# Reciprocals of the softmax sums: one transpose and copies by DMA in place of spread transposes and products

## The chip, the core and the metric

The kernel runs on one core of one Trainium2 chip. The core has five engines that run side by side, each in the order of its own instructions: TensorE (PE, with PEld for its weight loads), VectorE (DVE), ScalarE (ACT), GpSimd (POOL) and SyncE (SP, which here only issues DMA transfers). They wait for each other by semaphores. The metric is the device time of one execution in microseconds (us).

## What is computed

Attention with a position bias for 4 batches of 8 heads (576 tokens, 64 channels a head), then a first feed-forward layer with `g = h * cos(h)`, then a gated one with an RMS norm. The change lies in the attention:

```python
scores = scale * np.matmul(q, k.transpose(0, 1, 3, 2)) + bias
scores = scores - np.max(scores, axis=-1, keepdims=True)
attn = np.exp(scores)
attn = attn / (np.sum(attn, axis=-1, keepdims=True) + 1e-09)
return np.matmul(attn, v)
...
h = x @ w_in;  g = h * np.cos(h);  x = g @ w_out          # then RMS norm, SiLU gate, w_out
```

## The kernel before

**Units and steps.** The attention is cut into 16 units `u` (a pair of heads of one batch). A unit has five steps `p` = 0 to 4, and `step(u, p)` issues in this order: the score products of the step (`qk`, float32r, into the two PSUM tiles `psS`), then on VectorE `most` (adds the bias, takes the row's greatest value), then the transposes and copies of an earlier step, and on ScalarE `exps` (the exponential with the row sum). Steps 0 to 3 hold 128 query rows of each of the two heads, step 4 the last 64 rows of both heads together. That makes nine sums for a partition, `sum[:, 0:9]`.

**From scores to output.** `blocks` and `ninths` transpose the exponentials on TensorE into `pt` (three PSUM buffers), from where ScalarE and VectorE copy them to `eT`. `av(u, 0)` in step 3 multiplies them with `v` for the query rows of steps 0 and 1 ("half 0"), `av(w, 1)` in step 1 of the next unit (`w = u - 1`) those of steps 2 to 4 ("half 1"). The result `o` (one PSUM buffer) has channels on partitions and query rows along the free axis, 64 partitions for each head. So it can be divided by its sums only when 1/sum lies along the free axis too, the same in all 64 partitions of a head: this is the tile `rbc`. `norm_mul` multiplies `o` with `rbc` on VectorE: half 0 in `turn_end` (step 0 of the next unit), half 1 in step 2. `norm_split` then writes the two float32r parts `xh` (ScalarE) and `xl` (GpSimd).

**How rbc is made.** `recip(u, 0, 8)` in step 4 takes eight reciprocals on VectorE, and GpSimd widens each to 64 columns (`rw`, two copies). TensorE transposes `rw` in four pieces of 128x128 (L292), two in step 4 and two in the next step 0. `spread` copies each pair from PSUM to `rbc` on ScalarE (L308). The ninth reciprocal goes by `recip(u, 8, 9)` in `turn_end` and by two products with the identity (L319) ahead of `av(w, 1)`; `norm_tail` copies them (L342).

**What else stands near.** SP issues all loads in program order: `v` of the next unit (L361), weights `raw` for the later layers (L105, 512 KB, from unit 4), `rawk` and `rawq` of the next unit (`load`, L189), and in every fourth unit (3, 7, 11) nine bias loads (L215, L219). A DMA that waits for an engine holds all behind it on SP. The two layers that follow the attention (`run_item`) begin on TensorE at about 296 us.

Of the kernel before, what the change touches and what calls it, by code (L numbers as in the profile page):

```python
# [53 lines left out]
def attn_moe(tc, qd, kd, vd, smallp, lrow, ident_d, wf1, wf2, rmsg, out):  # L54
    nc = tc.nc
# [123 lines left out]

    raw_kq = {}  # L180

    def load(u):
        for k, src in enumerate((kd, qd)):
            if u == 0:
                t = rawp.tile([128, 512, 2], I32, tag="raw", name="first", bufs=NRAW)
                t = t.rearrange("p a b -> p (a b)")[:, 0:640].bitcast(F32)
            else:
                t = prep.tile([128, 640], F32, tag="raw" + "kq"[k], name="raw" + "kq"[k], bufs=1)
            nc.sync.dma_start(t, src[u % 4, u // 4])  # L189
            raw_kq[u, k] = t  # L190
        if u == 0:
            kq[0] = [raw_kq[0, 0], raw_kq[0, 1]]
# [70 lines left out]
    def exps(u, j):  # L263
        s_ = st[u]
        e2 = s_["e"][j // 2]
        e = e2[:, S * (j % 2):S * (j % 2) + S]
        nc.scalar.activation(e, e, AF.Exp, bias=s_["m"][:, j:j + 1], scale=-1.0, accum_out=s_["sum"][:, j:j + 1])  # L267
        if j == 8:
            nc.gpsimd.tensor_copy(e2[:, S:S + 64], e2[:, S - 64:S])
# [15 lines left out]
    def ninths(u, ps, half=None):  # L285
        s_ = st[u]
        pt = psA.tile([128, 512], F32, tag="tr", name="pt", bufs=3)
        for i, p in enumerate(ps):
            nc.tensor.transpose(pt[:, 128 * i:128 * i + 128], s_["e"].pop(p)[:, 512:640], ident)  # L289
        if half is not None:  # L290
            for i in range(0, 256, 128):
                nc.tensor.transpose(pt[:, 256 + i:384 + i], s_["rw"][:, 256 * half + i:256 * half + i + 128], ident)  # L292

        def out(copy):
            if ps[0] == 0:
                copy(s_["eT", 0][:, 8, 0:256], pt[:, 0:256])
            else:
                q0 = 128 * (ps[0] - 2)
                copy(s_["eT", 1][:, 8, q0:q0 + 128], pt[:, 0:128])

        def small(copy):
            for r0 in (0, 64):
                r = slice(r0, r0 + 64)
                copy(s_["eT", 1][r, 8, 256:320], pt[r, 128 + r0:192 + r0])

        def spread():
            rbc = ap.tile([128, 320], F32, tag="rbc", name="rbc", bufs=2)
            nc.scalar.copy(rbc[:, 0:256], pt[:, 256:512])  # L308
            s_["rbc", half] = rbc
        return out, small, spread  # L310

    def av(u, half):
        s_ = st[u]
        n = 256 if half == 0 else 320
        eT = s_["eT", half]
        o = s_["o"] = psA.tile([128, 512], F32, tag="o", name="o", bufs=1)
        if half == 1:
            for hh in range(2):
                nc.tensor.matmul(o[64 * hh:64 * hh + 64, 320:384], s_["r"][:, 8:9].to_broadcast([128, 64]),  # L319
                                 ident[:, 64 * hh:64 * hh + 64], start=True, stop=True, tile_position=(0, 64 * hh))  # L320
        vt = vts[u]
        for c in range(5):
            for hh in ((0, 1) if c % 2 else (1, 0)):
                nc.tensor.matmul(o[64 * hh:64 * hh + 64, 0:n], vt[:, c, 64 * hh:64 * hh + 64],  # L324
                                 eT[:, 2 * c + (hh if c < 4 else 0), :], start=(c == 0), stop=(c == 4),
                                 tile_position=(0, 64 * hh))

    def recip(u, a, z):  # L330
        s_ = st[u]
        nc.vector.tensor_scalar(s_["sum"][:, a:z], s_["sum"][:, a:z], 1e-9, None, op0=ALU.add)
        nc.vector.reciprocal(s_["r"][:, a:z], s_["sum"][:, a:z])
        if a == 0:
            rw = s_["rw"] = ap.tile([128, 512], F32, tag="rw", name="rw", bufs=1)
            for i in range(0, 8, 4):
                nc.gpsimd.tensor_copy(rw[:, 64 * i:64 * i + 256].rearrange("p (a b) -> p a b", b=64),
                                      s_["r"][:, i:i + 4].unsqueeze(2).to_broadcast([128, 4, 64]))

    def norm_tail(u):  # L340
        s_ = st[u]
        nc.scalar.copy(s_["rbc", 1][:, 256:320], s_["o"][:, 320:384])  # L342

    def norm_mul(u, half):
        s_ = st[u]
        n = 256 if half == 0 else 320
        xt = s_["xt"] = ap.tile([128, 320], F32, tag="xt", name="xt", bufs=1)
        nc.vector.tensor_tensor(xt[:, 0:n], s_["o"][:, 0:n], s_["rbc", half][:, 0:n], op=ALU.mult)

    def norm_split(u, half):  # L350
        hp, b = divmod(u, 4)
# [6 lines left out]
    def start_unit(u):  # L358
        hp, b = divmod(u, 4)
        vt = ap.tile([128, 5, 128], F32, tag="v", name="v", bufs=2)  # L360
        nc.sync.dma_start(vt, vd[b, hp])  # L361
        vts[u] = vt
        sm = ap.tile([128, 32], F32, tag="sm", name="sm", bufs=2)
        st[u] = {
            "m": sm[:, 0:9], "sum": sm[:, 10:19], "r": sm[:, 20:29], "e": {},
        }

    def turn_end(u, *now):
        a, b, c = blocks(u, 3, 0), blocks(u, 3, 1), blocks(u, 4, 0)
        out, small, spread = ninths(u, (3, 4), 1)  # L370
        recip(u, 8, 9)
        norm_mul(u, 0)
        a(nc.scalar.copy)
        if now:
            exps(now[0], 0)
        c(nc.scalar.copy)
        b(nc.vector.tensor_copy)
        out(nc.scalar.copy)
        small(nc.vector.tensor_copy)
        if now:  # L380
            exps(now[0], 1)
        spread()
        norm_split(u, 0)

    def convert(n):
# [4 lines left out]
    def step(u, p):  # L390
        hp, b = divmod(u, 4)
        w = u - 1
        if p == 0:
            start_unit(u)
        pss = qk(u, p)
        if p == 4:
            recip(u, 0, 8)
            if u >= 4:
                convert(1)
        for j, ps in enumerate(pss, 2 * p):  # L400
            most(u, j, ps)
            if b == 3:
                load_bias(hp + 1, j)
        if p == 0:
            if u >= 4:
                w_tick(lambda i: False)
            turn_end(w, u)
            if u > 1:
                split_q(u, 4)
            if u < 15:  # L410
                load(u + 1)
        elif p == 1:
            if w >= 0:
                av(w, 1)
            else:
                c0, c1 = blocks(u, 0, 0), blocks(u, 0, 1)
                c0(nc.vector.tensor_copy)
            exps(u, 2)
            exps(u, 3)
            if u == 0:  # L420
                c1(nc.scalar.copy)
            if u >= 4:
                convert(2)
            if w >= 0:
                norm_tail(w)
        elif p == 2:
            cs = [blocks(u, i, k) for i in range(1 if u == 0 else 0, 2) for k in range(2)]
            out, _, _ = ninths(u, (0, 1))
            if u >= 4:
                w_tick(lambda i: i < WA + WB, 1, False)  # L430
            cs.pop(0)(nc.scalar.copy)
            cs.pop(0)(nc.scalar.copy)
            exps(u, 4)
            if w >= 0:
                norm_mul(w, 1)
            for c in cs:
                c(nc.vector.tensor_copy)
            out(nc.scalar.copy)
            exps(u, 5)
            if 0 < u < 15:  # L440
                split_k(u + 1)
        elif p == 3:
            if 0 < u < 15:
                split_q(u + 1, 0)
            av(u, 0)
            if w >= 0:
                norm_split(w, 1)
            exps(u, 6)
            exps(u, 7)
            if u >= 4:  # L450
                convert(1)
        else:
            c0, c1 = blocks(u, 2, 0), blocks(u, 2, 1)
            out, _, spread = ninths(u, (2,), 0)
            if 0 < u < 15:
                split_q(u + 1, 1)
            c0(nc.scalar.copy)
            exps(u, 8)
            c1(nc.vector.tensor_copy)
            out(nc.scalar.copy)  # L460
            spread()
            if 0 < u < 15:
                split_q(u + 1, 2)
                split_q(u + 1, 3)
# [14 lines left out]
    nc.vector.memset(halfpi, float(math.pi / 2))  # L479
    nc.scalar.activation(cv[:, 0:1], halfpi, AF.Relu)  # L480
    nc.vector.memset(cv, 0.0)
    nc.vector.tensor_scalar(nbp, psi, b1s, -1.0, op0=ALU.mult, op1=ALU.mult)
    nc.gpsimd.tensor_scalar(w2s, w2s, 8.0, None, op0=ALU.mult)
    nc.scalar.activation(psb, psi, AF.Identity, scale=b1s)
# [347 lines left out]

    def rest():
        av(15, 1)
        norm_tail(15)

    turn_end(15)
    run_item(0, rest)
    def rest_out():
# [84 lines left out]
```

## Time and profile before

| what | value |
|---|---|
| median of 3 runs | 1150.82 us (1150.66 to 1151.09) |
| the profiled execution | 1150.9 us, its span in the trace 1149.1 us |
| mean granted TensorE clock | 0.999 of full speed |
| busy in the span | PE 1140.8, DVE 803.9, ACT 547.5, POOL 444.4 us |
| one unit in steady state | 15.5 us |

The span is what the trace covers; 1.8 us of the execution lie around it. A "busy" engine is one that has an instruction running; several TensorE instructions overlap in its pipeline, so what one costs is read from the start of it to the start of the next.

### The profile page before, as it was taken

To read this page: it belongs to the slowest core of one execution; us is meant where nothing else is said; L and a number is where in the kernel's file an instruction comes from. 1 tells how busy PE (TensorE), PEld (TensorE's weight loads), DVE (VectorE), ACT (ScalarE), POOL (GpSimd) and SP (SyncE) were. 2 spreads that over 40 slices of the span, in tenths; PEclk is the share of its full clock that TensorE was granted. 3 is DMA by queue.
4 is the path that set the end of the run, shared out by engine and by line. 5 is a ranking of instruction groups with operands and counts; after the bars stand their busy time and mean duration, and the time that the engine had idled before them with its cause. 6 is when DMAs were issued, how large, how long until landed. Compare 5 with 4: busy or idle time off the path is not lost.

```text
span 1149.1 us, 18558 instructions
## 1 busy us (share of the span) xinstructions
PE 1140.8 (99%) x6982; PEld 918.7 (80%) x6982; DVE 803.9 (70%) x1526; ACT 547.5 (48%) x1106; POOL 444.4 (39%) x555
## 2 busy tenths in 40 slices
PE   9999999999999999999999999999999999999998
PEld 4577777777788888888888887888888888888887
DVE  8867888888797798698778998685556355543232
ACT  8977788887653444354455555332322222122111
POOL 0245576665242352243244457553421241133111
PEclk9999999999999999999999999999999999999999
DMA  7925343442011011011101101011111011100111
GB/s 249 297 75 170 104 156 120 158 148 72 21 55 37 19 55 56 19 37 57 54 19 37 55 1 56 19 55 41 52 56 56 22 53 55 56 1 1 37 62 67
DMA packets 30682, 79.28 MB, mean 69 GB/s; under 512 B 3872, under 2 KB 4128, under 8 KB 30592
## 3 DMA queue, kind: packets, MB, share of 16 engines
q1 hardware_dynamic: 30400, 77.65, 21.4%
q8 instruction: 55, 0.90, 0.3%
q14 instruction: 35, 0.29, 0.1%
q10 hardware_dynamic: 144, 0.29, 0.1%
q0 software_dynamic: 48, 0.15, 0.1%
HBM read 62.47 MB, written 15.61 MB: 68 GB/s over the span
## 4 chain that ended last, share of the span: by engine, by line
PE 93%; ACT 2%; DVE 2%; POOL 1%; issue 1%; DVEq 0%; POOLq 0%; ACTq 0%
PE y L618 28%; PE h L618 17%; PE hv L618 12%; PE hg L618 12%; PE o L324 7%; PE psS L244 7%; PE pt L281 6%; PE psb L545 2%; ACT G L554 1%; PE pt L289 1%; PE pt L292 1%; DVE sq L734 0%; POOL wC L148 0%; PE o L319 0%; ACT ft L495 0%
## 5 line engine op out<-in xcount | busy, mean ns | idle before, releaser
L685 POOL TENSOR_TENSOR g<-t,g 128x512 fp32r<-128x512 f32 (+1 forms) x60 | 75.1, 1252 | 293.2 <-ACT g L684 293.2
L668 POOL TENSOR_TENSOR g<-t,g 128x512 fp32r<-128x512 f32 (+1 forms) x80 | 97.7, 1221 | 234.9 <-ACT g L667 234.9
L680 DVE TENSOR_TENSOR t<-t,hg 128x512 f32<-128x512 f32 (+1 forms) x60 | 38.0, 633 | 136.1 <-ACT t L679 136.1
L258 DVE CUSTOM_DVE_ANT_0 e<-psS,bias 128x576 f32<-128x576 f32 x144 | 103.9, 755 | 40.7 <-PE psS L244 35.0
L618 PE MATMUL y<-g,wB 128*128 128x512 f32 (+1 forms) x600 | 132.0, 369 | 0.0
L618 PEld LDWEIGHTS y<-g,wB 128*128 128x128 f32 x600 | 104.8, 189 | 19.1 <-POOL g L668 0.3
L267 ACT ACTIVATE e<-e,sm 128x576 f32<-128x576 f32 x144 | 112.0, 779 | 5.1 <-DVE sm L258 4.1
L679 ACT ACTIVATE t<-hg 128x512 f32<-128x512 f32 (+1 forms) x60 | 33.3, 554 | 169.2 <-PE hg L618 159.0
L684 ACT CAST g<-t 128x512 fp32r<-128x512 f32 (+1 forms) x60 | 34.7, 578 | 162.0 <-DVE t L683 162.0
L618 PE MATMUL h<-xh,wB 128*128 128x512 f32 (+1 forms) x360 | 109.1, 369 | 0.0
L618 PE MATMUL hv<-xh,wB 128*128 128x512 f32 (+1 forms) x320 | 97.2, 369 | 1.4 <-DVE t L666 1.4
L662 ACT ACTIVATE r<-r 128x512 f32<-128x512 f32 (+1 forms) x80 | 47.2, 589 | 105.7 <-DVE r L659 105.3
L618 PE MATMUL hg<-xh,wB 128*128 128x512 f32 (+1 forms) x320 | 96.8, 368 | 0.0
L618 PE MATMUL y<-wB,g 128*128 128x512 f32 x378 | 91.4, 389 | 0.0
L667 ACT CAST g<-t 128x512 fp32r<-128x512 f32 (+1 forms) x80 | 46.2, 578 | 94.6 <-DVE t L666 85.6
L324 PE MATMUL o<-eT,v 128*64 128x256 f32 (+1 forms) x640 | 83.9, 408 | 0.0
L618 PEld LDWEIGHTS y<-wB,g 128*128 128x128 f32 x378 | 70.5, 188 | 14.3
L244 PE MATMUL psS<-kt,qt 64*128 64x288 f32 (+1 forms) x810 | 79.7, 309 | 0.0
L618 PE MATMUL y<-g,wC 128*128 128x512 f32 (+1 forms) x360 | 79.7, 370 | 0.0
L244 PEld LDWEIGHTS psS<-kt,qt 64*128 64x128 f32 (+1 forms) x810 | 62.0, 185 | 20.7 <-issue 12.7
L683 DVE TENSOR_TENSOR t<-t,hv 128x512 f32<-128x512 f32 (+1 forms) x60 | 38.0, 633 | 57.6 <-PE hv L618 57.4
L666 DVE TENSOR_TENSOR t<-r,h 128x512 f32<-128x512 f32 (+1 forms) x80 | 50.3, 629 | 36.5 <-ACT r L663 36.1
(143 smaller groups left out, 2652.6 us busy)
## 6 DMA issues: line engine op xcount, KB each, us to landing
raw<-in_wf_dram SPq DMA_DIRECT2D x68, 512.0 KB, 3.6
bdram<-G SPq DMA_DIRECT2D x36, 295.5 KB, 4.6
bias<-bdram SPq DMA_DIRECT2D x32, 288.0 KB, 3.9
v<-in_vd_dram SPq DMA_DIRECT2D x16, 320.0 KB, 3.4
rawk<-in_kd_dram SPq DMA_DIRECT2D x15, 320.0 KB, 4.5
rawq<-in_qd_dram SPq DMA_DIRECT2D x15, 320.0 KB, 3.1
out_dram<-yacc SPq DMA_DIRECT2D x16, 256.0 KB, 2.1
bias<-bdram SPq DMA_DIRECT2D x4, 128.0 KB, 2.7
```

The costliest lines, as they stand in the source:

```text
L244: nc.tensor.matmul(ps[:, x, 0:288], qt[r, a, 128 * p:128 * p + 128], kt[r, b_, k0:k0 + 288], start=(n == 0), stop=(n == len(terms) - 1), t ...
L258: nc.vector.tensor_tensor_reduce(out=e.rearrange("p (a b) -> p a b", a=2), in0=ps[:, :, 0:288], in1=bias_t[j].rearrange("p (a b) -> p a b" ...
L267: nc.scalar.activation(e, e, AF.Exp, bias=s_["m"][:, j:j + 1], scale=-1.0, accum_out=s_["sum"][:, j:j + 1])
L281: nc.tensor.transpose(pt[:, 128 * i:128 * i + 128], e[:, k0:k0 + 128], ident)
L324: nc.tensor.matmul(o[64 * hh:64 * hh + 64, 0:n], vt[:, c, 64 * hh:64 * hh + 64], eT[:, 2 * c + (hh if c < 4 else 0), :], start=(c == 0), s ...
L618: nc.tensor.matmul(ps, a, b_, start=(first and k == 0), stop=(last and k == tot - 1))
L662: nc.scalar.activation(r, r, AF.Abs)
L666: nc.vector.tensor_tensor(t, r, ps, op=ALU.mult)
L667: nc.scalar.copy(g[:, 0, :tn], t)
L668: nc.gpsimd.tensor_tensor(g[:, 1, :tn], t, g[:, 0, :tn].bitcast(F32), op=ALU.subtract)
L680: nc.vector.tensor_tensor(t, t, pg, op=ALU.mult)
L685: nc.gpsimd.tensor_tensor(g[:, 1, :tn], t, g[:, 0, :tn].bitcast(F32), op=ALU.subtract)
```

## The change

Each half takes its reciprocals in one piece: `recip(u, 0)` (four sums, at the end of step 1) and `recip(u, 1)` (five sums, ahead of the next unit's step 0). They go into `rs[half]`, 16 or 20 columns with a reciprocal in every fourth. One transpose turns `rs[half]` to 16 or 20 rows of 128; it stands behind those of the exponentials in step 2 (half 0) and in the next step 0 (half 1). ScalarE copies these rows to `row`. SP then issues DMAs that read one row of `row` and write it to 64 partitions of `rbc[half]`: four for half 0, six for half 1. `load` is split, so that `rawk` is issued ahead of half 1's copies and `rawq` behind them. The widening on GpSimd, the four 128x128 transposes, the two products and their copies are gone.

```diff
-    def load(u):
-        for k, src in enumerate((kd, qd)):
+    def load(u, which=(0, 1)):
+        for k in which:
+            src = (kd, qd)[k]
...
         if half is not None:
-            for i in range(0, 256, 128):
-                nc.tensor.transpose(pt[:, 256 + i:384 + i], s_["rw"][:, 256 * half + i:256 * half + i + 128], ident)
+            n = 4 * (4 + half)
+            nc.tensor.transpose(pt[0:n, 256:384], rs[half], ident)
...
         def spread():
-            rbc = ap.tile([128, 320], F32, tag="rbc", name="rbc", bufs=2)
-            nc.scalar.copy(rbc[:, 0:256], pt[:, 256:512])
-            s_["rbc", half] = rbc
+            row = ap.tile([128, 128], F32, tag=f"row{half}", name="row", bufs=1)
+            nc.scalar.copy(row[0:n, :], pt[0:n, 256:384])
+            s_["row"] = row
...
-        if half == 1:
-            for hh in range(2):
-                nc.tensor.matmul(o[64 * hh:64 * hh + 64, 320:384], s_["r"][:, 8:9].to_broadcast([128, 64]),
-                                 ident[:, 64 * hh:64 * hh + 64], start=True, stop=True, tile_position=(0, 64 * hh))
...
+    rbc = [ap.tile([128, 256 + 64 * i], F32, name=f"rbc{i}") for i in range(2)]
+    rs = [ap.tile([128, 16 + 4 * i], F32, name=f"rs{i}") for i in range(2)]
...
+    def recip(u, half):
+        sums = s_["sum"][:, 4 * half:4 + 5 * half]
+        nc.vector.tensor_scalar(sums, sums, 1e-9, None, op0=ALU.add)
+        nc.vector.reciprocal(rs[half].rearrange("p (c z) -> p c z", z=4)[:, :, 0], sums)
...
+    def to_channels(u, half):
+        row = st[u]["row"]
+        for hh in range(2):
+            to = rbc[half][64 * hh:64 * hh + 64, :]
+            for p in range(2):
+                j = 4 * (2 * p + hh)
+                nc.sync.dma_start(to[:, 128 * p:128 * p + 128], row[j:j + 1, :].unsqueeze(1).to_broadcast([1, 64, 128]))
+            if half == 1:
+                nc.sync.dma_start(to[:, 256:320], row[16:17, 64 * hh:64 * hh + 64].unsqueeze(1).to_broadcast([1, 64, 64]))
...
     def turn_end(u, *now):
-        recip(u, 8, 9)
         norm_mul(u, 0)
...
         small(nc.vector.tensor_copy)
+        spread()
+        to_channels(u, 1)
         if now:
             exps(now[0], 1)
-        spread()
...
         if p == 0:
             start_unit(u)
+            if w >= 0:
+                recip(w, 1)
         pss = qk(u, p)
         if p == 4:
-            recip(u, 0, 8)
...
+            if u < 15:
+                load(u + 1, (0,))
             turn_end(w, u)
             if u > 1:
                 split_q(u, 4)
             if u < 15:
-                load(u + 1)
+                load(u + 1, (1,))
...
-            if w >= 0:
-                norm_tail(w)
+            recip(u, 0)
...
             out(nc.scalar.copy)
+            spread()
+            to_channels(u, 0)
             exps(u, 5)
...
+    for t in rs:
+        nc.vector.memset(t, 0.0)
```

On TensorE, from the last transpose of unit 1's step 4 to step 2 of unit 2, there stand before (`psS` scores, `pt` transposes, `o` the product with `v`):

```order
L289 MATMUL pt<-ident,e 128x128
L292 MATMUL pt<-ident,rw 128x128 x2
L244 MATMUL psS<-kt,qt 128x288 x12
L281 MATMUL pt<-ident,e 128x128 x12
L289 MATMUL pt<-ident,e 128x128 x2
L292 MATMUL pt<-ident,rw 128x128 x2
L244 MATMUL psS<-kt,qt 128x288 x12
L319 MATMUL o<-ident,sm 64x64 x2
L324 MATMUL o<-eT_1251,v 64x320 x10
L244 MATMUL psS<-kt,qt 128x288 x12
L281 MATMUL pt<-ident,e 128x128 x16
L289 MATMUL pt<-ident,e 128x128 x2
```

and at the same place after:

```order
L290 MATMUL pt<-ident,e 128x128
L245 MATMUL psS<-kt,qt 128x288 x12
L282 MATMUL pt<-ident,e 128x128 x12
L290 MATMUL pt<-ident,e 128x128 x2
L293 MATMUL pt<-ident,rs_94 20x128
L245 MATMUL psS<-kt,qt 128x288 x12
L322 MATMUL o<-eT_1263,v 64x320 x10
L245 MATMUL psS<-kt,qt 128x288 x12
L282 MATMUL pt<-ident,e 128x128 x16
L290 MATMUL pt<-ident,e 128x128 x2
L293 MATMUL pt<-ident,rs_93 16x128
```

Four transposes and two products have gone, and two transposes of 16 and 20 columns have come, one of them in step 2, where there was none.

On SP, from `v` of unit 4 to `v` of unit 5, there stand before:

```order
L361 DMA v<-in_vd_dram 128x640
L105 DMA raw<-in_wf_dram 128x1024 x2
L189 DMA rawk<-in_kd_dram 128x640
L189 DMA rawq<-in_qd_dram 128x640
L361 DMA v<-in_vd_dram 128x640
```

and after:

```order
L364 DMA v<-in_vd_dram 128x640
L105 DMA raw<-in_wf_dram 128x1024 x2
L190 DMA rawk<-in_kd_dram 128x640
L343 DMA rbc_92<-row 64x1x128 x2
L345 DMA rbc_92<-row 64x1x64
L343 DMA rbc_92<-row 64x1x128 x2
L345 DMA rbc_92<-row 64x1x64
L190 DMA rawq<-in_qd_dram 128x640
L343 DMA rbc_91<-row 64x1x128 x4
L364 DMA v<-in_vd_dram 128x640
```

Ten copies a unit stand between the loads: the six of half 1 behind `raw` and `rawk`, ahead of `rawq`, and the four of half 0 ahead of the next `v`.

On VectorE, at the seam between two units (unit 7 and 8), there stand before:

```order
L258 ISA e,sm<-psS,bias_1715 128x576
L258 ISA sm 128x1
L283 COPY eT_2668<-pt 128x4x128
L258 ISA e,sm<-psS,bias_2459 128x576
L258 ISA sm 128x1
L258 ISA e,sm<-psS,bias_2462 128x576
L258 ISA sm 128x1
L332 TENSOR_SCALAR sm<-sm 128x1
L333 RECIPROCAL sm<-sm 128x1
L348 TENSOR_TENSOR xt<-o,rbc 128x256
```

and after:

```order
L259 ISA e,sm<-psS,bias_1731 128x576
L259 ISA sm 128x1
L284 COPY eT_2692<-pt 128x4x128
L334 TENSOR_SCALAR sm<-sm 128x5
L335 RECIPROCAL rs_94<-sm 128x5
L259 ISA e,sm<-psS,bias_2479 128x576
L259 ISA sm 128x1
L259 ISA e,sm<-psS,bias_2482 128x576
L259 ISA sm 128x1
L351 TENSOR_TENSOR xt<-o,rbc_91 128x256
```

The two short instructions of the reciprocals have moved from behind the two `most` of step 0 to ahead of them.

## Rows read from the trace of the kernel before

**Rows 1.** The page: busy time of each engine, share of the span, instructions.
```profile
PE 1140.8 (99%) x6982; PEld 918.7 (80%) x6982; DVE 803.9 (70%) x1526; ACT 547.5 (48%) x1106; POOL 444.4 (39%) x555
```

**Rows 2.** Waits of PE, 50 to 310 us: us in total, times, longest.
```profile
PE pt L281 <- ACT e L267: 0.3, 1, 0.3
```

**Rows 3.** Timeline of PE, units 9 and 10: start, us, line, shapes, count.
```profile
200.71 0.27 PE L289 MATMUL pt<-ident,e 128*128 128x128 f32 x1
200.81 0.38 PE L292 MATMUL pt<-ident,rw 128*128 128x128 f32 x2
201.13 1.07 PE L244 MATMUL psS<-kt,qt 64*128 64x288 f32 x12
...
203.49 0.40 PE L289 MATMUL pt<-ident,e 128*128 128x128 f32 x2
...
204.04 1.06 PE L244 MATMUL psS<-kt,qt 64*128 64x288 f32 x12
205.03 0.34 PE L319 MATMUL o<-ident,sm 128*64 128x64 f32 x4
205.20 2.86 PE L324 MATMUL o<-eT,v 128*64 128x320 f32 x20
...
210.80 0.43 PE L289 MATMUL pt<-ident,e 128*128 128x128 f32 x2
211.16 1.05 PE L244 MATMUL psS<-kt,qt 64*128 64x288 f32 x12
212.15 2.38 PE L324 MATMUL o<-eT,v 128*64 128x256 f32 x20
```

**Rows 4.** Weight loads of L292 and of L319: ns min/median/max, forms.
```profile
L292 PEld LDWEIGHTS pt<-ident,rw x64: 138/140/143, 60.6 to 296.3; 128*128 128x128 f32 x64
...
L319 PEld LDWEIGHTS o<-ident,sm x64: 132/134/135, 65.1 to 299.5; 128*64 128x64 f32 x64
```

**Rows 5.** Timeline of all engines, unit 10: its VectorE and ScalarE.
```profile
201.66 0.19 ACT L267 ACTIVATION_READ_ACCUMULATOR e<-e,sm 128x1 f32 x1
...
202.22 0.76 DVE L258 CUSTOM_DVE_ANT_0 e<-psS,bias 128x576 f32<-128x576 f32 x1 [0.62 <-PE psS L244]
...
203.76 0.16 DVE L333 RECIPROCAL sm<-sm 128x1 f32<-128x1 f32 x1
...
204.53 0.28 ACT L299 COPY eT<-pt 128x128 f32<-128x128 f32 x1
...
209.19 0.76 DVE L258 CUSTOM_DVE_ANT_0 e<-psS,bias 128x576 f32<-128x576 f32 x1 [1.50 <-PE psS L244]
...
210.55 0.48 DVE L348 TENSOR_TENSOR xt<-o,rbc 128x320 f32<-128x320 f32 x1
...
210.95 1.28 DVE L283 COPY eT<-pt 128x512 f32<-128x512 f32 x2
```

**Rows 6.** Timeline of SP: start, us over all, line, count of issues.
```profile
23.79 7.00 SPq L556 DMA_DIRECT2D bdram<-G  x7
...
107.47 1.73 SPq L219 DMA_DIRECT2D bias<-bdram  x3
...
157.93 0.36 SPq L189 DMA_DIRECT2D rawk<-in_kd_dram  x1
```

**Rows 7.** Transfers by line: count, KB each, median us from issue to landing.
```profile
bias<-bdram SPq DMA_DIRECT2D x1, 16.0 KB, 2.5
...
bias<-bdram SPq DMA_DIRECT2D x4, 16.0 KB, 3.1
...
rawk<-in_kd_dram SPq DMA_DIRECT2D x1, 320.0 KB, 6.0
```

**Rows 8.** Timeline of all engines, units 4 and 7.
```profile
117.18 0.48 DVE L348 TENSOR_TENSOR xt<-o,rbc 128x320 f32<-128x320 f32 x1
...
118.23 0.72 POOL L195 CAST kt<-rawk 128x640 fp32r<-128x640 f32 x1 [3.86 <-DMA rawk<-in_kd_dram]
...
163.88 0.48 DVE L348 TENSOR_TENSOR xt<-o,rbc 128x320 f32<-128x320 f32 x1
```

More of the change, by code (lines that the diff above doesn't have):

```diff
@@ L326, in av @@
                                  tile_position=(0, 64 * hh))
-    def recip(u, a, z):
+    rbc = [ap.tile([128, 256 + 64 * i], F32, name=f"rbc{i}") for i in range(2)]
+    rs = [ap.tile([128, 16 + 4 * i], F32, name=f"rs{i}") for i in range(2)]
+    def recip(u, half):
         s_ = st[u]
[L332 to L342, printed above, removed]
+        sums = s_["sum"][:, 4 * half:4 + 5 * half]
[10 more added lines that the diff above has]
+                nc.sync.dma_start(to[:, 256:320], row[16:17, 64 * hh:64 * hh + 64].unsqueeze(1).to_broadcast([1, 64, 64]))
     def norm_mul(u, half):
@@ L347, in norm_mul @@
         xt = s_["xt"] = ap.tile([128, 320], F32, tag="xt", name="xt", bufs=1)
-        nc.vector.tensor_tensor(xt[:, 0:n], s_["o"][:, 0:n], s_["rbc", half][:, 0:n], op=ALU.mult)
+        nc.vector.tensor_tensor(xt[:, 0:n], s_["o"][:, 0:n], rbc[half][:, 0:n], op=ALU.mult)
     def norm_split(u, half):
@@ L364, in start_unit @@
         st[u] = {
-            "m": sm[:, 0:9], "sum": sm[:, 10:19], "r": sm[:, 20:29], "e": {},
+            "m": sm[:, 0:9], "sum": sm[:, 10:19], "e": {},
         }
@@ L423, in step @@
                 convert(2)
-            if w >= 0:
-                norm_tail(w)
+            recip(u, 0)
         elif p == 2:
             cs = [blocks(u, i, k) for i in range(1 if u == 0 else 0, 2) for k in range(2)]
-            out, _, _ = ninths(u, (0, 1))
+            out, _, spread = ninths(u, (0, 1), 0)
             if u >= 4:
@@ L453, in step @@
             c0, c1 = blocks(u, 2, 0), blocks(u, 2, 1)
-            out, _, spread = ninths(u, (2,), 0)
+            out, _, _ = ninths(u, (2,))
             if 0 < u < 15:
@@ L460, in step @@
             out(nc.scalar.copy)
-            spread()
             if 0 < u < 15:
@@ L834, in rest @@
         av(15, 1)
-        norm_tail(15)
+    recip(15, 1)
     turn_end(15)
```

## The prediction, made before the changed kernel ran

> **What bounds the kernel now.** I read the page first. TensorE is busy for 99% of the span, VectorE for 70%, the others for less than half [rows 1]. The waits come next: between 50 and 310 us, which hold all 16 units, TensorE waits once, for 0.3 us [rows 2]. So the attention goes at TensorE's pace, and whatever it no longer issues comes off the time, as long as no other engine falls behind. The timeline of TensorE gives the prices [rows 3], and the timelines of the others [rows 5, 8] show how late each of them may be. VectorE, ScalarE and GpSimd all have pauses in a unit. I work out one unit in steady state (unit 10, whose step 0 begins at 201.13) and multiply.
>
> **TensorE, the term that I trust most.** Costs go from start to start.
> - Step 4: one transpose of exponentials and two of `rw` take 201.13 - 200.71 = 0.42 us. Step 2 shows a stretch with none of `rw`: two transposes and the change to the score products, 211.16 - 210.80 = 0.36. A transpose is 200.81 - 200.71 = 0.10, so one and the change are 0.26. Step 4 saves 0.16.
> - Step 0: 204.04 - 203.49 = 0.55 for two and two. It becomes 0.36 + x, where x is a new transpose: saved 0.19 - x.
> - Step 1: the two products (four records) go: 205.20 - 205.03 = 0.17 saved.
> - Step 2 gets a new transpose: lost x.
>
> Together 0.52 - 2x a unit. No row shows x: 128 moving columns on 16 or 20 weight columns. The nearest above is the full transpose, 0.10; the nearest below is a record of the products with 64 and 64 columns, 0.17/4 = 0.04. I take the middle, 0.07: 0.38 us a unit, and 16 units make **6.1 us** (5.1 at x = 0.10, 7.0 at 0.04).
>
> The weight loads of 128 and of 64 columns last 140 and 134 ns [rows 4], so as latencies they hardly tell the two apart. [...]
>
> **VectorE, ScalarE and GpSimd.** The reciprocals of half 1 move ahead of `most` of step 0. They wait for the last exponential's sum, 201.66 + 0.19 = 201.85 [rows 5], and the two short instructions take some 0.35 (a reciprocal is 0.16 [rows 5], the addition ahead of it about the same). That ends at 202.20; the `most` behind them began at 202.22 after 0.62 us of waiting for its scores [rows 5]. The gap covers them, price 0. But the scores come 0.16 earlier now, and `most` can't follow: both end near 203.7 as before, and TensorE's step 1 wants to begin at 204.04 - 0.16 - 0.12 = 203.76. The cover is then used up: a reciprocal later by 0.1 would cost 0.1 a unit, 1.6 in all, and that is my bound. The reciprocals of half 0 fall into the 1.50 us pause ahead of 209.19 [rows 5]: nothing. On ScalarE a copy of 16 or 20 rows takes the place of a wider one, and `norm_tail` is gone; on GpSimd the two widening copies are gone. None of them was waited for by TensorE: no gain, no loss. The two memsets at the start come once.
>
> **The DMA, the term that decides.** Half 1 has a deadline in its own unit. Its row can be copied once `out` of step 0 has ended, 204.53 + 0.28 = 204.8 [rows 5]; with the copy, and TensorE 0.2 to 0.3 earlier, it is there at about 204.9, and the first copy is issued at 205.0. SP's nearest issues, to 64 partitions, are three in 1.73, 0.58 each [rows 6]: the sixth goes out at 207.9. The nearest transfer is the 16 KB bias piece, 64 partitions of 256 bytes: 2.5 us alone, 3.1 in the median of four [rows 7]. So half 1 lands at 210.4 (at 211.0 with 3.1).
>
> It is wanted by `norm_mul`, 210.55 before [rows 5] and some 0.45 sooner after (steps 4, 0 and 1): 210.1. What is queued behind it on VectorE are the two copies to `eT` (from 210.95, 0.64 each), and for the first of those waits TensorE's `av` of step 3, at 212.15 [rows 3]. 210.95 + 0.64 = 211.6 leaves some 0.45 to spare. Half 1 must land by 210.55, then: in time by 0.15, late by 0.45 at the upper end, which over 15 units is 6.8 us. I take "in time" (the lone transfer is the nearer row, since the copies read no DRAM). Half 0 has from 212 to the next unit's 219 and is free. `rawq` goes behind the six copies, at about 208, when it was held by GpSimd until 208 before: nothing.
>
> Three units have no such luck, since all SP transfers share one queue. In unit 4 `raw` goes out twice and `rawk` behind it; GpSimd gets `rawk` only at 118.2, after 3.86 us of waiting [rows 8]. The copies lie behind it, while `norm_mul` ran at 117.18 [rows 8] and must do so by 117.6 less the shift: 1.5 us lost. In unit 7 the bias loads push `rawk` to 157.93 + 6.0 = 163.9 [rows 6, 7], and `norm_mul` is due at 163.88 + 0.45 [rows 8]; the copies land 0.5 to 1 later: 0.5 lost, and the same in unit 11. Together **2.5 us** (1 to 4).
>
> Sum: -6.1 + 2.5 = -3.6 us. From the profiled execution's 1150.9 (span 1149.1 and 1.8 around it; the median is 1150.82, so the two agree): **1147.2 us**.
>
> **The rivals.**
> - *Every unit is late by half a microsecond* (landing at 3.1 and a bit): +6.8 more, 1154. It begins from a landing of 2.65 us behind the last issue. For it: the median of four. Against it: 2.5 for the lone one. Between this and the forecast, at 0.1 to 0.2 late a unit, lies no change.
> - *The copies hold each other up; slower by much.* All 64 reads of a copy go to one partition, and no row shows such a source. If a copy can't begin until the one ahead is through, its own time takes the place of the issue's 0.58. The nearest row of copies at a long pitch is `bdram`, seven in 7.00, 1.0 each [rows 6]: the last lands at 205.0 + 5 x 1.0 + 2.5 = 212.5, 1.95 late, 29 us over 15 units: 1176. It decides from a pitch of 0.61 on. [...]
> - *The change doesn't shorten TensorE*, because the VectorE chain of step 0 (exponential, reciprocal, two `most`) takes over: the savings of steps 4 and 0 go, that of step 1 stays less x, 0.1 x 16 = 1.6, and the three units cost less: 1150, no change. Against it: the ends meet to within 0.1 us.
>
> **How the numbers follow.** A measurement of this kernel tells about 0.2% from no change, 2.3 us. The forecast, half 1 in time but in three units, spans 1143.5 (x at 0.04, the three units for nothing: 1143.9, and 0.02 us of reading a unit) to 1148.5: chance 0.50. No change, by units that are late by 0.1 to 0.2 or by the VectorE chain: 0.20. Late by half a microsecond, to 1160: 0.14. Copies held up, beyond 1160: 0.16, left out. The range for 8 in 10 is so 1143.5 to 1160; faster 0.50, same 0.20, slower 0.30.
>
> **What would show it.** Right: TensorE's step 4 stretch at 0.26, step 1 without the 0.17, a unit of 15.1 us in place of 15.5, and waits of TensorE for `xt` or `eT` in units 4, 7 and 11 alone. Wrong: VectorE's `norm_mul` of half 1 with idle time ahead of it that ends on the DMA of `rbc` in every unit, and TensorE's `av` of step 3 behind it. Then SP's row tells which rival: issues 0.5 apart and a long landing, or landings that drift further from their issue with each of the six. A VectorE chain shows as TensorE waiting for `psS` at step 1.

## The result: 0.8% slower, and the profile after

| what | before | after |
|---|---|---|
| median of 5 runs | 1150.66 us (1150.35 to 1151.09) | 1159.97 us (1158.93 to 1162.84) |
| profiled execution, its span | 1150.9, 1149.1 us | 1158.93, 1157.1 us |
| mean granted TensorE clock | 0.999 | 0.999 |

The ratio of after to before is 1.0082 (95% interval 1.0071 to 1.0094): 9.3 us slower. The forecast was 3.6 us faster; the time lies at the very upper end of the range, 1160.0. All times are medians of undisturbed executions; one execution of the first kernel with loads behind the copies took 2905 us and is left out.

The page of after, busy time of each engine, answers to [rows 1]:

```profile
PE 1137.6 (98%) x6886; PEld 913.2 (79%) x6886; DVE 809.6 (70%) x1528; ACT 540.4 (47%) x1090; POOL 435.9 (38%) x523
```

TensorE is busy for 3.2 us less, in a span that is 8.0 us longer. It has begun to wait. Waits of PE, 50 to 310 us (us in total, times, longest), as in [rows 2]:

```profile
PE o L322 <- DVE eT L284: 11.1, 14, 2.3
PE pt L282 <- ACT e L268: 0.3, 1, 0.3
```

L322 is `av`, L284 the copy to `eT`: `av` of step 3 now waits in 14 units, where nothing waited before. The rest of this section reads one plain unit, then one with a backlog.

**TensorE's stretches.** Timeline of PE, from the end of unit 7 to step 3 of unit 8 (start, us, line, shapes, count), to hold against [rows 3]:

```profile
174.04 0.27 PE L290 MATMUL pt<-ident,e 128*128 128x128 f32 x1
174.25 1.07 PE L245 MATMUL psS<-kt,qt 64*128 64x288 f32 x12
...
176.61 0.41 PE L290 MATMUL pt<-ident,e 128*128 128x128 f32 x2
176.85 0.27 PE L293 MATMUL pt<-ident,rs 128*20 128x128 f32 x1
177.06 1.06 PE L245 MATMUL psS<-kt,qt 64*128 64x288 f32 x12
178.04 2.91 PE L322 MATMUL o<-eT,v 128*64 128x320 f32 x20
...
183.71 0.43 PE L290 MATMUL pt<-ident,e 128*128 128x128 f32 x2
183.97 0.27 PE L293 MATMUL pt<-ident,rs 128*16 128x128 f32 x1
184.17 1.06 PE L245 MATMUL psS<-kt,qt 64*128 64x288 f32 x12
```

Step 4 takes 174.25 - 174.04 = 0.21 where it took 0.42. Step 0 takes 177.06 - 176.61 = 0.45 (before 0.55). Step 1 takes 178.04 - 177.06 = 0.98 (before 1.16 up to `av`, 204.04 to 205.20). Step 2 takes 184.17 - 183.71 = 0.46 (before 0.36). That is 0.21 + 0.10 + 0.18 - 0.10 = 0.39 us less; `av` of 320 columns takes 0.05 more (2.84 from 178.04 to the next start at 180.88, before 2.79). Some 0.34 a unit is left: TensorE's part of the forecast is there.

**A plain unit.** Timeline of all engines in unit 9, the way of half 1's reciprocals (what stands in brackets is idle time of the engine just before, and what ended it); `row` is made at L309, its six copies are L343 and L345, `norm_mul` is L351:

```profile
193.09 0.28 ACT L300 COPY eT<-pt 128x128 f32<-128x128 f32 x1
193.40 0.46 DVE L305 COPY eT<-pt 64x64 f32<-64x64 f32 x2
193.90 0.25 ACT L309 COPY row<-pt 20x128 f32<-20x128 f32 x1 [0.53 <-DVE eT L305]
194.18 1.11 SPq L343 DMA_DIRECT2D rbc<-row  x2
195.34 0.59 SPq L345 DMA_DIRECT2D rbc<-row  x1
195.97 1.24 SPq L343 DMA_DIRECT2D rbc<-row  x2
197.25 0.59 SPq L345 DMA_DIRECT2D rbc<-row  x1
...
199.71 0.49 DVE L351 TENSOR_TENSOR xt<-o,rbc 128x320 f32<-128x320 f32 x1 [0.73 <-DMA rbc<-row]
200.12 1.28 DVE L284 COPY eT<-pt 128x512 f32<-128x512 f32 x2
200.85 2.38 PE L322 MATMUL o<-eT,v 128*64 128x256 f32 x20 [0.18 <-DVE eT L284]
```

ScalarE is free at 193.37 and copies the row only at 193.90: it waits for VectorE's two small copies (L305), which read the same tile `pt` and stand ahead of the row in the code. The trace has this wait in all 16 units. The total, among ScalarE's waits (50 to 310 us; us, times, longest):

```profile
ACT row L309 <- DVE eT L305: 8.4, 16, 0.5
```

Then the last of the six copies is issued 197.25 - 194.18 = 3.07 after the first. It lands 2.3 later by the trace, and `norm_mul` begins 2.46 after its issue. VectorE waits 0.73 for it, and the copies to `eT` and `av` behind it are late. Without a wait `av` begins 0.99 after the scores of step 2 [rows 3], here at 199.61 + 0.99 = 200.60; it begins at 200.85, 0.25 late.

**A unit with a backlog.** Timeline of all engines in unit 4 (kernel after), to hold against [rows 8]:

```profile
110.84 0.90 SPq L105 DMA_DIRECT2D raw<-in_wf_dram  x2
111.85 0.38 SPq L190 DMA_DIRECT2D rawk<-in_kd_dram  x1
113.00 1.26 SPq L343 DMA_DIRECT2D rbc<-row  x2
...
116.97 0.46 SPq L345 DMA_DIRECT2D rbc<-row  x1
...
120.62 0.49 DVE L351 TENSOR_TENSOR xt<-o,rbc 128x320 f32<-128x320 f32 x1 [2.84 <-DMA rbc<-row]
...
121.76 2.38 PE L322 MATMUL o<-eT,v 128*64 128x256 f32 x20 [2.27 <-DVE eT L284]
```

1.3 MB of loads lie ahead of the copies. `rawk`, the last of them, lands 7.6 us after its issue, and all six copies land behind it, the last one 1.1 us later. `norm_mul` waits 2.84 us for the copies and TensorE 2.27. The same row of `av` in units 7, 11 and 12 (timeline of PE):

```profile
169.96 2.38 PE L322 MATMUL o<-eT,v 128*64 128x256 f32 x20 [1.82 <-DVE eT L284]
...
233.31 4.07 PE L322 MATMUL o<-eT,v 128*64 128x256 f32 x20 [1.68 <-DVE eT L284]
...
251.65 2.38 PE L322 MATMUL o<-eT,v 128*64 128x256 f32 x20 [1.39 <-DVE eT L284]
```

That makes 7.16 us in four units, of 11.1 in all. The other ten lose 3.9 together, none over 1.0. `raw` and `rawk` stand ahead of the copies in most of those, too, but mostly go out earlier: in unit 9 5.3 and 4.9 us ahead of the first copy, in unit 7, where bias loads hold them, 1.4 and 0.9.

**One fall of TensorE's clock.** Windows of PE and the others (us; busy and instructions of PE, PEld, DVE, ACT, POOL; granted clock; DMA share, GB/s), ahead of and during `av` of unit 11, and during `av` of unit 4:

```profile
230.60:233.30 2.70, 1.03 (x13) 0.80 (x12) 1.14 (x3) 1.83 (x7) 2.25 (x2) 1.00 0.80 238
233.30:237.20 3.90, 3.89 (x20) 2.11 (x20) 3.22 (x7) 1.63 (x4) 3.08 (x5) 0.56 0.87 254
...
121.76:124.10 2.34, 2.34 (x21) 1.38 (x21) 1.90 (x5) 1.03 (x3) 2.18 (x6) 1.00 0.78 107
```

In unit 11 TensorE stood still for 1.68 us of the first window at a granted clock of 1.00; in the second it is 0.56, and the 20 products take 4.07 us where they take 2.38 elsewhere. That is 1.69 us more.

Against the kernel without copies in the first experiment below, after's profiled execution is 1158.93 - 1145.24 = 13.7 us longer. 11.1 are waits for `eT`, 1.7 the clock. For the 0.9 left there is only an estimate: in unit 9 the wait shown (0.18) falls short of the delay (0.25) by 0.07, and 14 times that is 1.0.

### The profile page after: what moved, and what is told of

Same layout as the page of the kernel before. It is cut to its first block, busy times and chain, and to the rows that moved or that the text cites. A ratio compares the mean times of both kernels' runs of the same rounds, so it can differ in the third digit from the quotient of the medians.

```text
span 1157.1 us, 18618 instructions
## 1 busy us (share of the span) xinstructions
PE 1137.6 (98%) x6886; PEld 913.2 (79%) x6886; DVE 809.6 (70%) x1528; ACT 540.4 (47%) x1090; POOL 435.9 (38%) x523
## 4 chain that ended last, share of the span: by engine, by line
PE 79%; DVE 5%; DMA 5%; ACT 3%; SPq 3%; issue 2%; POOL 2%; DVEq 0%; ACTq 0%; POOLq 0%
PE y L626 28%; PE h L626 16%; PE hv L626 12%; PE hg L626 12%; PE o L322 3%; DMA rbc<-row 3%; PE psS L245 3%; SPq L343 2%; PE psb L553 2%; PE pt L282 2%; DMA raw<-in_wf_dram 1%; DVE eT L284 1%; ACT e L268 1%; ACT G L562 1%; SPq L345 1%
## 5 line engine op out<-in xcount | busy, mean ns | idle before, releaser
L322 PE MATMUL o<-eT,v 128*64 128x256 f32 (+1 forms) x640 | 86.4, 417 | 11.1 <-DVE eT L284 11.1
L322 PEld LDWEIGHTS o<-eT,v 128*64 128x64 f32 x640 | 43.9, 139 | 43.8 <-DVE eT L284 14.5
```

## The experiments

Each was timed against runs of the kernel before on the same chip (medians 1150.61 to 1150.76). Theory A: TensorE saves what was forecast, and all that is lost comes from half 1's copies landing late, in every unit by the row's wait for VectorE, and in four units by loads ahead of them. Rival B: TensorE did not get shorter, or the extra DMA traffic slows something else. Rival C: the copies hold each other up at their source.

### The change without its copies

```diff
-        to_channels(u, 1)
...
-            to_channels(u, 0)
...
+    for t in rbc:
+        nc.gpsimd.memset(t, 1.0 / 576)
```

> The changed kernel without its DMA copies from row to rbc; rbc holds 1/576 once, so the division by the sums is left out. Late landing: TensorE's waits for eT (11.1 us) and the 1.7 us at a granted clock of 0.56 in unit 11 go, a unit is 15.2 to 15.3 us in all 15, and the time is 1150.7 - 16 x 0.3 = 1145 to 1146.5. Rival, TensorE's own order costs more than read (a new transpose at 0.10, slower changes between kinds of products) or the VectorE chain of step 0 takes over: 1149 or more with no DMA at all.

1145.34 us (1145.24 to 1145.37), ratio 0.9953 (0.9938 to 0.9967). Waits of PE, 50 to 310 us:

```profile
PE pt L282 <- ACT e L268: 0.3, 1, 0.3
```

`rbc` holds a constant here; all other instructions of the engines are still there, and the wait for `eT` has gone. So the change's own work is worth 1150.76 - 1145.34 = 5.4 us, and the copies take back 1159.97 - 1145.34 = 14.6. The half of B by which TensorE did not get shorter falls. This kernel leaves out the copies of both halves, but `norm_mul` of half 0 never waits in after, so the loss is that of half 1.

### The row ahead of the small copies

```diff
-        small(nc.vector.tensor_copy)
         spread()
         to_channels(u, 1)
+        small(nc.vector.tensor_copy)
```

> The changed kernel with the copy of the row ahead of VectorE's two small copies. Late landing by a late start: ScalarE no longer waits 0.53 us for VectorE ahead of the row's copy, the first DMA of half 1 goes out some 0.5 sooner, and the stalls of 0.2 to 0.4 in units 1, 5, 6, 8, 9, 10, 13, 14, 15 go, 0.5 each in units 2 and 3: 3 to 4 us less than the changed kernel, about 1156. Units 4, 7 and 11, where the copies stand behind raw and rawk, keep theirs. Rival, the copies hold each other at their source: the same landings, only begun sooner, and the same gain, but landings of half 1 longer than 2.8 us. Rival, the start doesn't matter: 1160.

1155.94 us (1155.63 to 1156.55), ratio 1.0044 (1.0027 to 1.0061): 4.0 us faster than after. Waits of PE, 50 to 310 us:

```profile
PE o L322 <- DVE eT L284: 9.1, 9, 3.5
```

Nine units wait in place of 14. Of what is left, units 4, 7, 11 and 12 have 3.49 + 1.51 + 1.51 + 0.96 = 7.5 us, and in unit 4 `av` behind the wait takes 3.97, where it takes 2.38 in unit 8. The wait at the tile `pt` has only changed sides: VectorE's small copies now wait for the row (waits of DVE, 50 to 310 us).

```profile
DVE eT L305 <- ACT row L309: 4.3, 16, 0.4
```

So it is the order of the two readers in the code that decides which of them waits. ScalarE's wait for VectorE is one cause, worth 4 of the 14.6 us, and not the larger one.

### Loads behind the copies, two ways that failed

`raw` and `rawk` were issued behind half 1's six copies, in the kernel as changed:

```diff
         if p == 0:
             if u >= 4:
-                w_tick(lambda i: False)
+                w_tick(lambda i: False, fetch=False)
+            turn_end(w, u)
+            if u >= 4:
+                w_fetch()
+                wstate["dmad"] = wstate["dma"]
             if u < 15:
                 load(u + 1, (0,))
-            turn_end(w, u)
```

> The changed kernel with raw and rawk issued behind half 1's six copies. Queue order: the stalls of units 4, 7, 11 and 12 (2.29, 1.83, 3.36, 1.41 beyond a unit of 15.26) fall to the 0.2 to 0.4 of the others, 7 to 8 us less than the changed kernel, about 1152; landings of half 1 are 2.8 us in all units. Rival, the traffic itself slows the copies whatever their place: those units keep 1 us or more and the time stays above 1156.

1171.55 us (1171.06 to 1171.63, three executions), ratio 1.0179 (1.0162 to 1.0196): 12 us slower than after, where 7 to 8 us faster were expected. There is no trace of these three. The next kernel has the same edit together with the row ahead of the small copies, and its trace shows a cause:

> Both edits, row first and loads behind. If late start and queue order are the whole of the loss, no unit stalls and the time is that of the kernel without copies, 1145 to 1147. If something else is left (landing of 2.8 us per copy at the issue pitch of 0.63), 0.1 to 0.3 a unit stays: 1148 to 1150.

1162.49 us (1162.27 to 1163.73), ratio 1.0104 (1.0089 to 1.0119). Waits, 50 to 310 us, the largest of POOL and those of PE:

```profile
POOL kt L200 <- DMA rawk<-in_kd_dram: 73.1, 14, 8.2
...
PE psS L249 <- POOL qt L200: 9.9, 9, 2.0
...
PE o L326 <- DVE eT L288: 2.9, 5, 1.1
```

Timeline of all engines, unit 4's `rawk` and the scores behind it:

```profile
121.14 0.72 POOL L200 CAST kt<-rawk 128x640 fp32r<-128x640 f32 x1 [8.23 <-DMA rawk<-in_kd_dram]
...
123.42 0.30 POOL L200 CAST qt<-rawq 128x128 fp32r<-128x128 f32 x1
123.77 1.33 PE L249 MATMUL psS<-kt,qt 64*128 64x288 f32 x12 [2.05 <-POOL qt L200]
```

The wait for `eT` fell to 2.9 us, from 9.1 with the row alone, but `rawk` now comes so late that GpSimd splits the keys, and behind them the first queries, after TensorE wants them. These two waits of TensorE are 12.8 of the some 17 us by which this kernel lies above the one without copies; where the rest is, is not shown. I had counted `rawk` as free to move. It is not: `rawk` has a deadline on GpSimd, while `raw`, for the later layers, has none of this kind in the unit. That gave the next kernel.

### Only raw behind the copies

```diff
             if u >= 4:
-                w_tick(lambda i: False)
+                w_tick(lambda i: False, fetch=False)
...
                 load(u + 1, (1,))
+            if u >= 4:
+                w_fetch()
+                wstate["dmad"] = wstate["dma"]
```

with the row ahead of the small copies; `rawk` stays where the change put it.

> Row first, and only raw (512 KB) moved, behind rawq; rawk stays ahead of half 1's copies. If it is raw in the queue that makes half 1 late in units 4, 7, 11, 12, and rawk's lateness that made the run with both behind slow, then VectorE's waits for rbc fall under 2 us in all, GpSimd gets rawk and rawq in time, and the time is 1146 to 1148. If rawk's own 320 KB is enough to hold the copies: units 7 and 11 (bias loads, then rawk) keep 1 us each, 1149 to 1150. If raw now comes late for the weights: waits of ScalarE for raw, 1150 or more.

1148.48 us (1147.19 to 1149.97, 10 runs), ratio 0.9981 (0.9972 to 0.9990). Waits of PE, 50 to 310 us, and the loads of `rawk` by line (count, KB each, median us to landing):

```profile
PE o L326 <- DVE eT L288: 2.6, 5, 1.1
PE o L326 <- DVE xt L355: 0.4, 1, 0.4
...
rawk<-in_kd_dram SPq DMA_DIRECT2D x15, 320.0 KB, 3.8
```

7.5 us faster than the row alone, though 0.5 above what was expected (1146 to 1148): VectorE still waits 7.1 us for `rbc`, not under 2. `rawk` lands sooner, 3.8 us in place of 5.2 in after. In units 4, 7 and 11 TensorE's wait is gone. Unit 12 keeps 1.13 (0.96 with the row alone), so `raw` is not what makes that unit late; what does, no run here tells. `raw` ahead of the copies was the largest cause, and the order on SP's queue decides it, not the amount of traffic: every byte is still moved. With that the other half of B falls, too, but for the 3.1 us by which this kernel still lies above the one without copies.

### norm_mul behind the copies to eT

```diff
-            if w >= 0:
-                norm_mul(w, 1)
             for c in cs:
                 c(nc.vector.tensor_copy)
+            if w >= 0:
+                norm_mul(w, 1)
```

> The changed kernel with norm_mul of half 1 behind the two eT copies on VectorE in step 2 instead of ahead of them. Late landing: the two copies (1.28 us) no longer queue behind the wait, and TensorE's av of step 3 waits for o alone, some 0.65 us later than before: the plain units' stalls of 0.2 to 0.4 go and those of units 2, 3, 4, 7, 11, 12 shrink by about 0.65: 1152 to 1154. Rival, the wait only moves to o or to the step behind: 1158 or more.

In the kernel as changed: 1153.41 us (1151.93 to 1155.21, 10 runs), ratio 1.0023 (1.0014 to 1.0033). The late landings are still there, and no longer hold up `eT`; what `av` still waits for is `norm_mul` itself, which must have read `o` before `av` may write it. Waits of PE, 50 to 310 us:

```profile
PE o L322 <- DVE xt L351: 6.0, 7, 2.0
```

So 6.6 us of after's time go with the place of `norm_mul` on VectorE: two copies that need no reciprocal stood behind one instruction that did. This is no further share beside the 4.0 and 7.5 above; it takes the same lateness off at its other end. Together with the row first and `raw` last:

> The same with norm_mul of half 1 behind the two eT copies too. If landings are the whole of the loss, this has 0.65 us more to spare in each unit and reaches the kernel without copies, 1145.3 to 1146.5; no gain over the one before would mean that nothing was late there any more.

1146.50 us (1145.85 to 1147.53), ratio 0.9965 (0.9952 to 0.9978): faster than both kernels, by 4.1 and 13.5 us, and 1.2 us above the kernel without copies. Waits of PE, 50 to 310 us, and behind them a plain unit's half 1 in the timeline of all engines:

```profile
PE o L326 <- DVE xt L355: 0.4, 2, 0.3
```

```profile
186.24 0.25 ACT L313 COPY row<-pt 20x128 f32<-20x128 f32 x1
186.51 1.11 SPq L347 DMA_DIRECT2D rbc<-row  x2
...
189.59 0.59 SPq L349 DMA_DIRECT2D rbc<-row  x1
...
191.88 1.28 DVE L288 COPY eT<-pt 128x512 f32<-128x512 f32 x2
...
193.09 0.48 DVE L355 TENSOR_TENSOR xt<-o,rbc 128x320 f32<-128x320 f32 x1
193.62 2.38 PE L326 MATMUL o<-eT,v 128*64 128x256 f32 x20
```

Neither `norm_mul` nor TensorE's products wait here. The row first, `raw` last and `norm_mul` behind the copies together leave 0.4 us of TensorE's waiting for `norm_mul`; where the rest of the 1.2 us is, no run shows.

### The rows on neighbouring partitions

For C the reciprocals were put into neighbouring columns, so that the transposed rows lie on partitions 0 to 4 and not on every fourth. If the copies hold each other up at their source, they land later here and the time grows.

```diff
-            n = 4 * (4 + half)
+            n = 4 + half
...
-    rs = [ap.tile([128, 16 + 4 * i], F32, name=f"rs{i}") for i in range(2)]
+    rs = [ap.tile([128, 4 + i], F32, name=f"rs{i}") for i in range(2)]
...
-                j = 4 * (2 * p + hh)
+                j = 2 * p + hh
```

> The changed kernel with the reciprocals in neighbouring columns, so that the rows lie on neighbouring partitions 0 to 4 instead of every fourth. [...] If each copy's 2.8 us is its own (issue to receipt), landings stay and the time stays at 1160.

1171.42 us (1170.17 to 1173.13), ratio 1.0183 (1.0166 to 1.0200). Transfers by line (count, KB each, median us from issue to landing), first of after, then of this kernel:

```profile
rbc<-row SPq DMA_DIRECT2D x128, 32.0 KB, 2.8
...
rbc<-row SPq DMA_DIRECT2D x32, 16.0 KB, 2.4
```

```profile
rbc<-row SPq DMA_DIRECT2D x128, 32.0 KB, 3.9
...
rbc<-row SPq DMA_DIRECT2D x32, 16.0 KB, 3.4
```

Bytes, issues and targets of the copies are the same; of them only the source partitions differ, and in the median a copy lands 1.0 to 1.1 us later. The sign that the prediction named is a landing that drifts further from its issue with each copy. In after there is none: unit 9's six land 2.7, 2.8, 2.3, 2.8, 2.8 and 2.3 us after their issues. With neighbouring rows the four of half 0, issued from 87.74, land after 3.3, 3.9, 4.5 and 4.5: the first three are 1.1 to 1.2 us apart, where SP issues one in some 0.6. So copies do hold each other up when their rows are neighbours (3.9 us in the median), and with a row in every fourth partition they do not (2.8): C holds for this kernel and not for the change. The 32 KB copies read partitions 0 to 3 here. The 16 KB copies read partition 4 and are 1.0 us later as well; whether they wait behind the others in the queue, no run shows.

## Why the prediction was wrong

**Right.** TensorE bounds the kernel and what it no longer issues comes off: 5.4 us measured without the copies, 6.1 forecast. The one unknown price, the new transpose, was taken as 0.07; step 0 gives 0.45 - 0.36 = 0.09 and step 2 gives 0.10, the upper bound, where the sum was 5.1. The place of the danger was right as well: half 1's landing, `norm_mul`, the copies to `eT`, `av` of step 3; so were the landing of the last copy (2.5 forecast; in unit 9 2.3, and 2.46 until `norm_mul` begins), half 0, whose `norm_mul` never waits, and the price of nothing for `most` behind the reciprocals: TensorE never waits for `psS` in after. ScalarE and GpSimd cost TensorE nothing by their amount of work, either.

**Wrong, the step that turned the sign: "in time by 0.15".** It was built from the start of step 0. In unit 9 of after (step 0 at 189.69) the first copy is issued 4.49 us later, not 3.87: 0.62 late, of which 0.53 is ScalarE's wait for VectorE's small copies. The prediction took the row as ready for copying when ScalarE's own `out` had ended, and left out that another engine's copy of the same tile stands ahead of it. The diff showed that: `spread` moved from behind `exps` to right behind `small`. In the kernel before, the `exps` between them covered the wait (0.6 us there, once, against 8.4 after), and with the row first it was gone. The issues took 3.07, not 2.9: another 0.17. `norm_mul` begins 2.46 behind the last issue, not 2.5: 0.04 back. And the deadline was kinder than I put it, 199.46 against a computed 189.69 + 9.42 = 199.11, by 0.35: of the 0.45 by which I had moved it ahead, step 4's 0.16 lies ahead of step 0 and doesn't count from there, and the new transpose of step 2 (0.10) and a longer `av` of 320 columns (0.05) work the other way. Together 0.15 - 0.62 - 0.17 + 0.04 + 0.35 = -0.25: the delay measured in unit 9 (199.46 is worked back from that delay, so the sum has to close; its terms are what it tells). So plain units were the rival "late in every unit", at half its size; I gave it 0.14 and should have seen that a margin of 0.15 on five estimated terms carries no forecast.

**Wrong in size: the units with loads ahead of the copies.** 2.5 us (1 to 4) was forecast for units 4, 7 and 11; the waits there are 2.27 + 1.82 + 1.68, and unit 12 has 1.39 that I did not foresee: 7.16 together, and the granted clock of 0.56 in unit 11 adds 1.69. The clock has no term in the prediction. I took `rawk`'s landing from the kernel before and put the copies 0.5 to 1 us behind it. Both were short: `rawk` takes 6.8 us to land in unit 7 and 6.6 in unit 11, against 6.0 in both before (7.6 against 7.3 in unit 4), and the last copy lands 1.1 us behind it in all three. Moving `raw` alone behind the copies gave 7.5 us and freed these three units, but not unit 12. Unit 8 has the same order of loads as unit 12 and waits only 0.18; its last two copies land 2.8 and 2.4 us after their issues, those of unit 12 3.8 and 3.3.

**Luck.** That 1159.97 still lies inside the range, by 0.03, says nothing for the working: its upper end stands for half a microsecond in every unit, and the time came there by half of that and by loads that cost over three times their forecast (7.16 + 1.69 against 2.5). One sum has a slip: 1150.9 - 3.6 is 1147.3, not 1147.2, which changes nothing here.

**The other rivals.** "The copies hold each other up" was right in the wrong place: neighbouring rows showed it (a landing of 3.9 us), the rows of the change (2.8) did not. "The change doesn't shorten TensorE" is excluded by the kernel without copies. What the forecast named as its own refutation is what came: `norm_mul` with idle time ahead of it that ends on the DMA of `rbc`, and `av` behind it.

## What to carry to other kernels

When work goes from an engine to a DMA, its cost on the engine is easy to read and its cost as a latency decides: add up the chain from the last producer to the first consumer, with every instruction that reads or writes the same tile ahead of it on any engine, and every load ahead of it on the issuing queue. If the margin that comes out is smaller than the error of its terms, the place to look is behind the consumer: what stands there and doesn't need the data (here two copies to `eT`) should go first. And a load that nobody waits for soon (`raw`) goes behind the small transfers that somebody does wait for, while one with a consumer of its own (`rawk`) can't be moved so freely.

## What the runs showed of the hardware

- A transpose with 16 or 20 weight columns costs TensorE 0.09 to 0.10 us from start to start, like one with 128 (0.10). Its weight load alone is shorter, 0.09 us in the trace of after against 0.138 to 0.143 in [rows 4]. That is a third less for less than a sixth of the columns, and the time from start to start does not fall.
- A broadcast of one row to 64 partitions lands 2.8 us after its issue with 32 KB and 2.4 with 16 KB, and SP issues one in some 0.61 us (3.07 for five steps). Behind two loads of 512 KB and one of 320 KB on the same queue (unit 4 of after) the four of 32 KB take 4.7 to 6.6.
- TensorE's granted clock stayed at 1.00 over `av` behind a wait of 2.27 us (unit 4 of after) and was at 0.56 behind one of 1.68 (unit 11 of after). With neighbouring rows it was 0.55 over `av` behind a wait of 1.60, where the 20 products took 4.07 us; they took 4.02 behind 1.85, and 2.38 behind 1.68:

```profile
191.67 4.07 PE L322 MATMUL o<-eT,v 128*64 128x256 f32 x20 [1.60 <-DVE eT L284]
```

The length of the wait alone doesn't tell which of them is followed by a fall, so a wait that looks like 1.6 us can cost twice that (here 1.60 and, for the products, 4.07 - 2.38 = 1.69 more).
